# Attention and feed-forward on one core: the second chunk's units, moved one or two half steps back beside the first chunk

## The chip, the cores and the metric

The kernel runs on one core of a Trainium2 chip. The time is device microseconds (us) from one execution; a kernel's time is the median of several. The profiled execution is a single one, and its own time stands beside its span in the table below. A "clock" is the TensorE clock that the throttle granted, as a share of full speed.

Five engines work side by side, each through its own queue in order: TensorE (PE, with its weight loads as PEld), VectorE (DVE), ScalarE (ACT), GpSimd (POOL) and SyncE (SP), which here issues nearly all transfers. An instruction that waits holds everything behind it on its engine.

## The reference

Two parts follow each other. Attention: 8 batches, 8 heads of 64, 512 local tokens and 32 global ones. A local token sees the local tokens within 32 places and all global ones; a global token sees everything.

```python
s_ll = scale * np.matmul(q_l, k_l.transpose(0, 1, 3, 2))
s_ll = np.where(np.abs(pos[:, None] - pos[None, :]) <= 32, s_ll, -1e9)
a_l = sm(np.concatenate([scale * np.matmul(q_l, k_g.transpose(0, 1, 3, 2)), s_ll], axis=-1))
out_l = np.matmul(a_l, np.concatenate([v_g, v_l], axis=2))
```

Then, on the heads laid side by side (`x`, 8 x 576 x 512, in float32), a layer norm and a feed-forward with 2048 hidden columns:

```python
xn = (x - mu) / np.sqrt(var + 1e-06) * g_ln
return x + np.maximum(xn @ w_ch1, 0.0) @ w_ch2
```

## The kernel before

**Chunks and units.** The rows are cut into nine chunks: eight of 512 local rows (two halves of 256 rows each) and a last one with the 256 global rows. Chunk c's feed-forward runs on TensorE while the attention for chunk c+1 is computed in between. A local chunk's attention is eight units, one for each pair of heads and half. A unit has three parts: scores (16 small matmuls for each of two heads into two banks `sc`, L262; on VectorE the mask and row minimum, L275, four instructions; on ScalarE four exponentials, L285), transposes (four on TensorE into a bank `tp`, L299, with a copy `pt` on ScalarE, L301, for the first sixteen units; on VectorE, L307, for later ones), and values (32 matmuls into a bank `pv`, L316, a reciprocal, L327, and the scaled copy into `x` on VectorE, L328). `sc`, `tp`, `pv` and the chunk's transposes `t` (L492) share two banks. The fourth and eighth unit also finish a half: its rows are stored to DRAM (`xs`, L342) and normalised (BN_STATS L189, L191; on ScalarE L202).

**The feed-forward.** The hidden columns are cut into sixteen weights, called f0 to f15 here. For each there is a first product (`mm1`, L531, twelve 512-column matmuls into `ph`, as three passes: low weight times high x, high times low, high times high), then `hh` on ScalarE (L539) and `hl` on VectorE (L540), and a second product (`mm2`, L550, three matmuls for each of four row tiles into `acc`). `mm2` of f-1 follows `mm1` of f, so a chunk has 32 half steps: 2f is `mm1(f)`, 2f+1 is `mm2(f-1)`.

**The weights.** Beside the first chunk, each weight also arrives as a raw 64-bit tile (L165, 1 MB) and is split into a high and a low float32 part: ScalarE L138 and L139, VectorE L141, L142 and L146, ScalarE L150, VectorE L152. The raw buffers are few, so the transfer of a later weight waits until L146 of an earlier one has read its buffer. `weights_to` is called in each even half step and keeps the split four weights ahead in program order.

**What sets the order.** TensorE's queue is written out by hand from the first chunk on: `PLACES` gives for a chunk the start, the period and the offsets of a unit's three parts in half steps, and a part runs in the half step

```python
place = min(max(int(start + n * period) + o, place), 2 * NF - 1)
```

as soon as that half step's matmuls yield (three times in `mm1`, once for each row tile in `mm2`). SyncE's queue is written by hand too, in the program's order. VectorE's, ScalarE's and GpSimd's queues are ordered by a scheduler from its own costs, before the kernel runs.

Of the kernel before, what the change touches and what calls it, by code (L numbers as in the profile page):

```python
# [31 lines left out]

ON_PE = 16

PLACES = {0: (0, 3.5, (0, 2, 3)), 1: (0, 3.4, (0, 1, 4)), 7: (1, 3.5, (0, 1, 2)), 9: (1, 3.75, (0, 1, 4))}
BIG = 3.0e38


# [8 lines left out]
def attention_ffn_kernel(  # L47
# [679 lines left out]
    for c, chunk in enumerate(chunks):  # L727
# [8 lines left out]
        traced["units"] = want  # L736
        start, period, offs = PLACES.get(c, PLACES[9])
        at = {}
# [108 lines left out]
```

## Time and profile before

| | |
|---|---|
| median of 3 runs | 998.15 us (997.30, 998.15, 999.79) |
| profiled execution | 995.42 us, span 993.6 us, clock 0.983 |
| TensorE busy (matmuls) | 948.8 us, 95% |
| VectorE busy | 578.0 us, 58% |
| ScalarE busy | 314.7 us, 32% |
| raw weight transfers | 16 of 1024 KB, median 5.4 us from issue to landing |
| unit transfers (`u`) | 63 of 848 KB, median 4.7 us |

The first chunk's feed-forward stretches from about 58 to 176 us of the span. A row of the timeline has start, duration, engine, line, operation, result and operands, and in square brackets the idle time before it with what ended it. A row of the list of waits has engine, tile and line, what it waited for, and then us in total, times, longest. A piece of the chain of waits has start, duration, engine, tile and line.

### The profile page before, as it was taken

To read this page: it belongs to the slowest core of one execution; us is meant where nothing else is said; L and a number is where in the kernel's file an instruction comes from. 1 tells how busy PE (TensorE), PEld (TensorE's weight loads), DVE (VectorE), ACT (ScalarE), POOL (GpSimd) and SP (SyncE) were. 2 spreads that over 40 slices of the span, in tenths; PEclk is the share of its full clock that TensorE was granted. 3 is DMA by queue.
4 is the path that set the end of the run, shared out by engine and by line. 5 is a ranking of instruction groups with operands and counts; after the bars stand their busy time and mean duration, and the time that the engine had idled before them with its cause. 6 is when DMAs were issued, how large, how long until landed. Compare 5 with 4: busy or idle time off the path is not lost.

```text
span 993.6 us, 21066 instructions
## 1 busy us (share of the span) xinstructions
PE 948.8 (95%) x8616; PEld 717.2 (72%) x8616; DVE 578.0 (58%) x1873; ACT 314.7 (32%) x842; POOL 44.0 (4%) x150
## 2 busy tenths in 40 slices
PE   6569999999999999999999999999999989999997
PEld 4347677677777777777777777777777766766796
DVE  4589943666766666766666666766666642222311
ACT  5677743223222223222322222222222231232210
POOL 3000000000000000000000000000000000000000
PEclk9679999999999999999999999999999999999999
DMA  8565632323232224222332224222322344543110
GB/s 357 203 250 203 231 113 85 121 76 119 97 120 75 89 80 149 90 93 71 104 122 84 101 68 146 93 71 93 123 84 86 108 158 150 191 147 136 44 32 22
DMA packets 31872, 118.80 MB, mean 120 GB/s; under 512 B 4256, under 2 KB 6304, under 8 KB 27680
## 3 DMA queue, kind: packets, MB, share of 16 engines
q1 hardware_dynamic: 31776, 117.46, 34.6%
q8 instruction: 68, 1.11, 0.5%
q14 instruction: 28, 0.23, 0.1%
HBM read 99.62 MB, written 17.83 MB: 118 GB/s over the span
## 4 chain that ended last, share of the span: by engine, by line
PE 85%; DMA 3%; DVE 3%; ACT 2%; issue 1%; SPq 0%; POOL 0%; ACTq 0%; DVEq 0%
PE acc L550 37%; PE ph L531 36%; PE sc L262 4%; PE pv L316 3%; DMA raw<-in_wd 2%; PE t L492 1%; PE pv L419 1%; DMA xs<-x 1%; PE sc L371 1%; PE t L407 1%; DVE tmp L142 0%; DVE hl L540 0%; DVE pt L307 0%; DVE tmp L146 0%; ACT p L285 0%
## 5 line engine op out<-in xcount | busy, mean ns | idle before, releaser
L550 PE MATMUL acc<-w,hh 128*128 128x512 f32 x1088 | 342.7, 396 | 0.0
L531 PE MATMUL ph<-xh,w 128*128 128x512 f32 (+1 forms) x1216 | 311.7, 382 | 0.0
L307 DVE STREAM_TRANSPOSE pt<-p 32x128 f32<-32x128 f32 x768 | 232.5, 303 | 62.2 <-ACT p L285 50.1
L531 PEld LDWEIGHTS ph<-xh,w 128*128 128x128 f32 x1216 | 214.0, 188 | 49.8 <-issue 3.1
L550 PEld LDWEIGHTS acc<-w,hh 128*128 128x128 f32 x1088 | 205.7, 189 | 44.4
L550 PE MATMUL acc<-w,hl 128*128 128x512 f32 x544 | 225.7, 415 | 2.9 <-DVE hl L540 2.9
L539 ACT ACTIVATE hh<-ph 128x512 fp32r<-128x512 f32 (+1 forms) x144 | 82.3, 572 | 355.6 <-PE ph L531 354.4
L540 DVE SCALAR_TENSOR_TENSOR hl<-ph,hh 128x512 fp32r<-128x512 f32 (+1 forms) x144 | 94.3, 656 | 164.9 <-ACT hh L539 163.4
L285 ACT ACTIVATE p<-p,mn 128x128 f32<-128x128 f32 x256 | 99.7, 391 | 187.9 <-DVE mn L275 187.9
L531 PE MATMUL ph<-xl,w 128*128 128x512 f32 x512 | 143.4, 401 | 0.0
L550 PEld LDWEIGHTS acc<-w,hl 128*128 128x128 f32 x544 | 102.4, 188 | 32.7 <-issue 7.2
L531 PEld LDWEIGHTS ph<-xl,w 128*128 128x128 f32 x512 | 94.0, 188 | 27.8 <-issue 6.9
L275 DVE CUSTOM_DVE_ANT_0 p<-sc,mask 128x128 f32<-128x128 f32 x256 | 58.9, 285 | 45.4 <-PE sc L262 44.8
L262 PE MATMUL sc<-u 64*32 64x128 f32 x2048 | 58.1, 293 | 13.0 <-DMA u<-in_eu 6.2
L262 PEld LDWEIGHTS sc<-u 64*32 64x32 f32 x2048 | 32.3, 112 | 41.6 <-issue 25.1
L316 PEld LDWEIGHTS pv<-u,pt 128*32 128x32 f32 x2048 | 33.8, 113 | 28.1 <-issue 22.4
L328 DVE TENSOR_TENSOR x<-pv,ri 128x256 f32<-128x256 f32 x64 | 26.8, 420 | 43.6 <-PE pv L316 43.6
L316 PE MATMUL pv<-u,pt 128*32 128x64 f32 x2048 | 45.7, 228 | 3.1 <-ACT pt L301 3.0
L285 ACT ACTIVATION_READ_ACCUMULATOR p<-p,mn 128x1 f32 x256 | 47.9, 187 | 0.0
L326 POOL TENSOR_SCALAR ri<-sm 128x4 f32<-128x4 f32 x64 | 17.4, 272 | 585.1 <-ACT p L285 580.9
L202 ACT ACTIVATE x<-x,rs 128x512 f32<-128x512 f32 x32 | 24.8, 811 | 45.1 <-DMA xs<-x 43.5
L492 PE MATMUL t<-ident,x 128*128 128x128 f32 x136 | 23.1, 290 | 10.1 <-DVE x L207 3.9
(58 smaller groups left out, 442.0 us busy)
## 6 DMA issues: line engine op xcount, KB each, us to landing
u<-in_eu SPq DMA_DIRECT2D x63, 848.0 KB, 4.7
raw<-in_wd SPq DMA_DIRECT2D x16, 1024.0 KB, 5.4
gk<-in_gk SPq DMA_DIRECT2D x8, 1088.0 KB, 5.0
xs<-x SPq DMA_DIRECT2D x32, 256.0 KB, 5.7
ob<-xs SPq DMA_DIRECT2D x32, 256.0 KB, 3.4
out<-ob SPq DMA_DIRECT2D x32, 256.0 KB, 2.1
gv<-in_gv SPq DMA_DIRECT2D x8, 1024.0 KB, 5.0
u<-in_eu SPq DMA_DIRECT2D x1, 512.0 KB, 4.1
```

The lines of the kernel that those rows point to most:

```text
L202: nc.scalar.activation(x[:, j, :], x[:, j, :], AF.Identity, bias=rs[:, 1, j:j + 1], scale=rs[:, 0, j:j + 1],)
L262: nc.tensor.matmul(sc[h][gp, qb * P:(qb + 1) * P], self.e[hd, w * WIN:(w + 1) * WIN], self.e[hd, k0 * WIN:(k0 + 4) * WIN], start=True, sto ...
L275: nc.vector.tensor_tensor_reduce(out=self.p[:, c], in0=sc[h][:, qb * P:(qb + 1) * P], in1=masks[half, qb], scale=-QSCALE, scalar=BIG, op0= ...
L285: nc.scalar.activation(self.p[:, c], self.p[:, c], AF.Exp, bias=mn[:, c:c + 1], scale=-1.0, accum_out=self.sm[:, c:c + 1],)
L307: nc.vector.transpose(out=self.pt[rp, :, gp], in_=self.p[gp, :, rp])
L316: nc.tensor.matmul(pv[gp, qb * P + h * D:qb * P + h * D + D], self.pt[:, 2 * h + qb, gp], self.v[:, 4 * qb + g, h * D:(h + 1) * D], start= ...
L328: nc.vector.tensor_tensor(self.x[:, :, hp * P:(hp + 1) * P].rearrange("p q (h d) -> p q h d", h=2), pv[:, :256].rearrange("p (q h d) -> p ...
L492: nc.tensor.transpose(t[:, j * P:(j + 1) * P], xn[j][:, kt * P:(kt + 1) * P], ident)
L531: nc.tensor.matmul(ph[:, :n], w[:, kt, :], xx[kt][:, :n], start=(i == 0), stop=(i == 3 * KT - 1),)
L539: nc.scalar.activation(hh[:, :n], ph[:, :n], AF.Relu)
L540: nc.vector.scalar_tensor_tensor(hl[:, :n], ph[:, :n], 0.0, f32(hh[:, :n]), ALU.max, ALU.subtract)
L550: nc.tensor.matmul(acc[t], a[:, ts], w, start=(f == 0 and i == 0), stop=(f == NF - 1 and i == 2),)
```

## The change

One entry of the table is different: the first chunk's row, which places the units of the second chunk.

```diff
-PLACES = {0: (0, 3.5, (0, 2, 3)), 1: (0, 3.4, (0, 1, 4)), 7: (1, 3.5, (0, 1, 2)), 9: (1, 3.75, (0, 1, 4))}
+PLACES = {0: (2, 3.4, (0, 2, 3)), 1: (0, 3.4, (0, 1, 4)), 7: (1, 3.5, (0, 1, 2)), 9: (1, 3.75, (0, 1, 4))}
```

The scores of the eight units stood in half steps 0, 3, 7, 10, 14, 17, 21, 24 and now stand in 2, 5, 8, 12, 15, 19, 22, 25; transposes follow two and values three half steps later, as before. The scheduler gives VectorE and ScalarE another order in this chunk as a consequence; behind it, all queues are as they were. Three places follow, each first as it stood, then as it stands.

TensorE, from the last transposes of the chunk's own input (`t`) to the end of the first product of f0 (`ph` from `xh` and `xl`); `sc` are the scores of the first unit:

```order
L492 MATMUL t<-ident,x 128x128 x8
L262 MATMUL sc<-u 32x128 x16
L531 MATMUL ph<-xh_593,w 128x512 x2
L531 MATMUL ph<-xh_605,w 128x512 x2
L531 MATMUL ph<-xl_594,w 128x512 x2
L531 MATMUL ph<-xl_606,w 128x512 x2
L531 MATMUL ph<-xh_593,w 128x512 x2
L531 MATMUL ph<-xh_605,w 128x512 x2
L299 MATMUL tp<-ident,p 128x128 x4
```

```order
L492 MATMUL t<-ident,x 128x128 x4
L531 MATMUL ph<-xh_593,w 128x512 x2
L492 MATMUL t<-ident,x 128x128 x4
L531 MATMUL ph<-xh_605,w 128x512 x2
L531 MATMUL ph<-xl_594,w 128x512 x2
L531 MATMUL ph<-xl_606,w 128x512 x2
L531 MATMUL ph<-xh_593,w 128x512 x2
L531 MATMUL ph<-xh_605,w 128x512 x2
L262 MATMUL sc<-u 32x128 x16
```

The scores moved behind the first product, and two matmuls of that product now stand between the transposes.

VectorE, from an L142 of weight f4 to the scaled copy (L328) of the first unit's values. Before, `tmp_796` and `w_795` are f4 and `w_736` is f3; now `tmp_767` and `w_766` are f4 and `tmp_836` is f5; the `hl` are those of f0 and f1 before, of f1 and f2 now:

```order
L142 SCALAR_TENSOR_TENSOR tmp_796<-tmp_796,raw_745 128x1024
L146 SCALAR_TENSOR_TENSOR tmp_796<-raw_745,tmp_796 128x1024
L152 TENSOR_TENSOR w_736<-tmp_737,w_736 128x1024
L540 SCALAR_TENSOR_TENSOR hl_791<-ph_735,hh_790 128x512
L152 TENSOR_TENSOR w_795<-tmp_796,w_795 128x1024
L328 TENSOR_TENSOR x_829<-pv_830,ri_847 128x2x128
```

```order
L142 SCALAR_TENSOR_TENSOR tmp_767<-tmp_767,raw_745 128x1024
L327 RECIPROCAL ri_887<-ri_887 128x4
L540 SCALAR_TENSOR_TENSOR hl_819<-ph_765,hh_818 128x512
L146 SCALAR_TENSOR_TENSOR tmp_767<-raw_745,tmp_767 128x1024
L141 TENSOR_SCALAR tmp_836<-tmp_836 128x1024
L142 SCALAR_TENSOR_TENSOR tmp_836<-tmp_836,raw_747 128x1024
L152 TENSOR_TENSOR w_766<-tmp_767,w_766 128x1024
L540 SCALAR_TENSOR_TENSOR hl_866<-ph_834,hh_865 128x512
L146 SCALAR_TENSOR_TENSOR tmp_836<-raw_747,tmp_836 128x1024
L328 TENSOR_TENSOR x_869<-pv_870,ri_887 128x2x128
```

The three passes of f5 now stand ahead of the first unit's L328.

ScalarE, around the exponentials of the fifth unit (`p_1270` before, `p_1289` now). Before, `tmp_1427` is f12 and `tmp_1474` f13; now `tmp_1514` is f14 and `tmp_1604`, from `raw_1475`, is f15:

```order
L138 ACTIVATE tmp_1427<-raw_1266 128x1024
L139 ACTIVATE raw_1335<-raw_1335 128x1024
L138 ACTIVATE tmp_1474<-raw_1335 128x1024
L139 ACTIVATE raw_1435<-raw_1435 128x1024
L285 ACTIVATE p_1270,sm_1269<-p_1270,mn_1268 128x128 x4
L539 ACTIVATE hh_1309<-ph_1256 128x512
```

```order
L138 ACTIVATE tmp_1514<-raw_1382 128x1024
L150 CAST w_1466<-tmp_1467 128x1024
L285 ACTIVATE p_1289,sm_1288<-p_1289,mn_1287 128x128
L138 ACTIVATE tmp_1604<-raw_1475 128x1024
L285 ACTIVATE p_1289,sm_1288<-p_1289,mn_1287 128x128
L139 ACTIVATE raw_1475<-raw_1475 128x1024
L285 ACTIVATE p_1289,sm_1288<-p_1289,mn_1287 128x128 x2
```

The exponentials stood behind the work for f13; three of the four now stand behind a pass of f15, the last weight.

## The prediction

> **What bounds the kernel now.** I read the clock line first (the page's PEclk), then the three stretches of the first chunk, then TensorE's waits inside it, then the engines in order of time. The stretches, with columns time, busy time of PE, PEld, DVE, ACT, POOL, granted clock, DMA share, GB/s:
>
> ```profile
> 58.10:73.96 15.86, 13.50 (x137) 9.58 (x137) 15.23 (x33) 13.45 (x22) 0.39 (x1) 0.90 0.66 245
> 73.96:130.29 56.33, 52.92 (x457) 39.91 (x456) 52.80 (x95) 42.64 (x81) 4.62 (x7) 0.97 0.59 205
> 130.29:176.40 46.11, 46.11 (x363) 35.75 (x369) 16.82 (x42) 13.98 (x33) 1.39 (x4) 1.00 0.29 96
> ```
>
> 58.10 is where TensorE begins unit 1's scores, 176.40 where it ends the chunk's last matmul. Up to about 130 VectorE is as full as TensorE (15.23 of 15.86, 52.80 of 56.33), since it splits the weights; after that TensorE alone is full. So in the first two stretches either may end last, and in the third a delay of TensorE goes into the time one for one. TensorE's idle time there:
>
> ```profile
> PE sc L262 <- DVE xl L505: 3.9, 1, 3.9
> PE pv L316 <- ACT pt L301: 2.2, 4, 1.1
> PE sc L262 <- DVE x L328: 1.6, 3, 1.3
> PE tp L299 <- ACT p L285: 1.1, 1, 1.1
> PE acc L550 <- DVE hl L540: 0.8, 1, 0.8
> ```
>
> These rows hold all that a new order in this chunk could gain: 9.6 us, 3.9 of it ahead of unit 1's scores. Every row names an operation that queues on VectorE or ScalarE among the weights. The longest late one also costs clock:
>
> ```profile
> 121.24 0.40 PE L262 MATMUL sc<-u 64*32 64x128 f32 x2
> 122.91 1.10 PE L262 MATMUL sc<-u 64*32 64x128 f32 x30 [1.27 <-DVE x L328]
> 123.00:126.00 3.00, 3.00 (x35) 2.23 (x36) 2.97 (x11) 1.86 (x2) 0.00 (x0) 0.50 0.79 258
> ```
>
> After 1.27 us of idle the clock was 0.50 for three microseconds, worth about 1.4 us more (at 0.50, 3.0 us do the work of 1.5). No other chunk's order differs, so I cost this chunk only.
>
> **The change, part by part.** No instruction is added or removed; each of the eight units moves by one or two half steps. I write unit 1 to 8 for the second chunk's units and f0 to f15 for the weights.
>
> *The start gains.* These rows fix it:
>
> ```profile
> 58.10 1.50 PE L262 MATMUL sc<-u 64*32 64x128 f32 x32 [3.91 <-DVE xl L505]
> 56.29 0.83 ACT L504 ACTIVATE xh<-t,g_sb 128x256 fp32r<-128x256 f32 x2
> 57.57 0.87 DVE L505 SCALAR_TENSOR_TENSOR xl<-t,g_sb,xh 128x256 fp32r<-128x256 f32 x2
> 59.53 2.00 PE L531 MATMUL ph<-xh,w 128*128 128x512 f32 x4
> 76.76 0.60 PE L299 MATMUL tp<-ident,p 128*128 128x128 f32 x4
> ```
>
> The first product of f0 no longer stands behind unit 1's scores. It goes on when the last xh is there (57.1). Its eight matmuls up to the xl ones run cold at 0.46 each, as the row at 59.53 has them, and the last are warm: first product done near 61.1. The order from there costs, by these pieces of the chain of waits, 2.80 a product, 2.80 or 3.00 a group of twelve second-product matmuls, 0.60 scores, 0.58 values, 0.44 transposes:
>
> ```profile
> 136.93 0.60 PE sc L262 x32
> 137.52 3.00 PE acc L550 x12
> 140.52 2.80 PE ph L531 x12
> 143.32 0.44 PE tp L299 x4
> 146.56 0.58 PE pv L316 x32
> ```
>
> Scores to 61.75, f1's product to 64.75, f0's second product to 67.55. Unit 1's transposes wait for its exponentials: ScalarE holds them behind a weight operation that waits for f6's transfer until 65.17 (next fence; that transfer starts behind f2's L146, which does not move), then 1.03, a cast of 0.95 and four exponentials of 0.39: 68.7. Transposes to 69.2, f2's product to 72.0. Before, that point was 76.76, with 1.18 more done (unit 1's values, unit 2's scores): the new order is **3.6 us ahead**.
>
> *VectorE takes it back.* Passes of one weight; where nothing is waited for, the next instruction starts about a tenth of a microsecond before the listed end of the last, so I lay them from start to start:
>
> ```profile
> 65.17 1.16 ACT L139 ACTIVATE raw<-raw 128x1024 int32<-128x1024 uint16 x1 [0.34 <-DMA raw<-in_wd]
> 66.20 1.05 ACT L150 CAST w<-tmp 128x1024 fp32r<-128x1024 f32 x1
> 69.56 1.22 DVE L152 TENSOR_TENSOR w<-tmp,w 128x1024 fp32r<-128x1024 f32 x1
> 70.69 0.42 DVE L328 TENSOR_TENSOR x<-pv,ri 128x256 f32<-128x256 f32 x1
> 74.78 0.69 DVE L141 TENSOR_SCALAR tmp<-tmp 128x1024 f32<-128x1024 f32 x1
> 75.38 1.22 DVE L146 SCALAR_TENSOR_TENSOR tmp<-raw,tmp 128x1024 int32<-128x1024 int32 x1
> 76.52 1.22 DVE L142 SCALAR_TENSOR_TENSOR tmp<-tmp,raw 128x1024 int32<-128x1024 int32 x1
> 80.00 0.68 DVE L540 SCALAR_TENSOR_TENSOR hl<-ph,hh 128x512 fp32r<-128x512 f32 x1
> 88.22 0.28 DVE L275 CUSTOM_DVE_ANT_0 p<-sc,mask 128x128 f32<-128x128 f32 x1
> 60.27 1.23 DVE L142 SCALAR_TENSOR_TENSOR tmp<-tmp,raw 128x1024 int32<-128x1024 int32 x1
> ```
>
> A step is 0.60 for L141, 1.14 for L142, 1.13 for L146 and L152, 0.60 for hl, 0.85 for a unit's four L275, 0.35 for L328, 0.1 for the reciprocal. VectorE's order is the same until the last row ends at 61.41. From there it holds f2's L152 and f3's L146 (63.7), hl of f0 and the L275 (65.1), L141 of f4 (65.7); L152 of f3 waits for its cast until 67.15 and ends at 68.3; L142 of f4, reciprocal, hl of f1, L146 of f4 (71.3); then L141, L142 of f5, L152 of f4, hl of f2 and L146 of f5 (75.9), and only then unit 1's L328, 76.2. Unit 2's scores need the bank that it frees. TensorE is there at 73.5: **2.8 us idle**, where the row before was 0.18.
>
> On to L146 of f13: eight each of L141, L142, L146, L152 (32.0), four hl (2.4), three units' L275 (2.5), three L328 and reciprocals (1.4), 38.3 in all, and 1.65 of waits for casts and transfers: from 75.9 to 115.85. That frees the buffer of f15's transfer. In the old order it stood near 118.9, so the weights now run 3 us earlier against the units. Laying TensorE beside it I find idle 0.55 and 2.1 us at unit 2's transposes and values, 0.8 at unit 3's scores, 0.8 and 1.6 at unit 4's transposes and unit 5's scores; TensorE ends f8's product at 121.95.
>
> *Where it ends.* Unit 5's exponentials now stand in ScalarE's queue among f15's two passes. Durations:
>
> ```profile
> 64.68 4.77 DMA raw<-in_wd
> 95.67 8.71 DMA raw<-in_wd
> 121.05 1.13 ACT L138 ACTIVATE tmp<-raw 128x1024 f32<-128x1024 f32 x1
> 126.28 0.39 ACT L285 ACTIVATE p<-p,mn 128x128 f32<-128x128 f32 x1
> 130.29 0.48 PE L550 MATMUL acc<-w,hl 128*128 128x512 f32 x1
> ```
>
> The transfer of f15 starts at 115.9 and takes 4.8 to 8.7; at 5.3, near the shorter row, it lands at 121.2. L138 (1.05), an exponential (0.39), L139 (1.05), two exponentials (0.78): 124.5. Transposes of unit 5 follow 2.6 us late, end at 125.0; f7's second product (2.8), values (0.6), f9's product (3.0) and unit 6's scores (0.6) bring TensorE to f8's second product at **132.0**. Before, that was 130.29 with one set of transposes (0.44) more behind it: 129.85. So +2.2 us; all that follows is in the third stretch, where TensorE waits for nothing. VectorE's own bound, hl of f8 at 128.3, does not bind.
>
> Two unknown costs remain. Clock: the earlier stalls' slow clock is absorbed, as TensorE has 2.6 us in hand at unit 5's transposes; behind that stall it costs 0 to 1.4, and I take 0.7. The page "TensorE: Matmul & The Clock Gate" of the Trainium skill (Part 1, What's actually happening) puts the cold state behind at least one idle window of about 3.4 us. By that rule no stall here cools the array and the sum loses the 0.7; the row of 1.27 us speaks against it. Transfer: unit 6's 848 KB are queued 2.1 us ahead of f15; the 8.71 row is such a pair only 0.4 apart. I take 0.6, with 0 to 2.2 as bounds (8.71 - 4.77 - 1.7). **Sum: 2.2 + 0.7 + 0.6 = +3.5 us.** On the profiled execution (span 993.6, 995.42 us in all) that makes 998.9; the three runs' median, 998.15, lies 2.7 higher, so I forecast a median of **1001.6**.
>
> The moved loads cost nothing, and GpSimd's order is the same: unit 7's keys now wait in SyncE's queue behind the first residual load, and that behind L146 of f15 (127.7), so they land near 133.5, and the scores need them near 142. Were they late, TensorE would stop one for one.
>
> **Rivals.** *A, faster:* the head start survives. It needs VectorE and ScalarE to serve unit 2 to unit 5 with no more idle than before (2.2 + 1.6 us, less what the start removes). Then -3.6, so 994.5. For it: the weights are never what a product waits for. Against it: the laid order with L328 behind five weight passes. *B, no change:* the work of VectorE to hl of f8 is the same in both, and stalls only change place; my +2.2 without the unknown costs, less the two microseconds that hand-laid waits may err: 998 to 1000.5, say 999. *C, slower through the tail:* the last unit's values are now 8.4 us ahead of the transposes of the next chunk's input, three groups of 2.8, where the old order had 11.3.
>
> ```profile
> 156.89 0.65 PE L316 MATMUL pv<-u,pt 128*32 128x64 f32 x32
> 158.29 0.41 DVE L328 TENSOR_TENSOR x<-pv,ri 128x256 f32<-128x256 f32 x1
> 163.96 1.52 ACT L202 ACTIVATE x<-x,rs 128x512 f32<-128x512 f32 x2 [6.31 <-DMA xs<-x]
> 108.59 8.09 DMA xs<-x
> ```
>
> Values to L328 0.1, L328 0.45, store to landing 5.2, normalising 1.5: 7.3, so 1.1 us is left. Where the store takes 8.1, as the earlier one did, it is 1.8 late: 1003.4, the forecast with 1.8 on top. DMA is idle enough there (0.29) to make that unlikely.
>
> **How the numbers follow.** Forecast 0.46, A 0.18, B 0.24, C 0.12. A measurement of this kernel tells about 0.3% (3 us) from none. The forecast's own range is 999 to 1005 (costs 0 to 3.6, waits 2 either way); it lies above 1001.1 two times in three (0.30), C nearly always (0.11), B one time in ten (0.02): slower 0.43. A is faster nine times in ten: 0.17. The rest, 0.40, is within. The range 994.5 to 1006 takes in the forecast with its unknown costs, B, and C beside the forecast's centre; it leaves out half of A and C on top of a dear forecast.
>
> **What would show it.** In the new profile: f0's first product before unit 1's scores, ended near 61; a wait of unit 2's scores for L328 of 2 to 4 us near 74; a wait of unit 5's transposes for the exponentials of 1 to 4 us near 123; TensorE's idle after the first product, up to f8's second product, at 10 to 14 us (12.5 as laid, unit 1's transposes with 1.2 among them) instead of 5.7, the four lower rows of the list of waits; f8's second product at 131 to 135; no idle after it. A wait for xl that stays, f8's second product before 129, or idle ahead of the chunk's last transposes would make me wrong.

## The result, and the profile after

| | before | changed |
|---|---|---|
| median | 998.67 us (995.30 to 1000.31) | 1004.74 us (1003.20 to 1005.43) |
| profiled execution | 995.42 us, span 993.6 us | 1003.66 us, span 1001.8 us |
| TensorE's mean clock | 0.983 | 0.977 |

The changed kernel takes 1.0061 times the time of the kernel before, with an interval of 1.0036 to 1.0085: 0.6%, or 6 us, slower. A second measurement beside later experiments gave 1006.33 us and 1.0086 [1.0060, 1.0111].

Three stretches of the changed kernel answer, roughly, to the three of before (the first ends at unit 2's scores here, just behind them there): from unit 1's scores to unit 2's, to f8's second product, to the next chunk's scores (columns as before).

```profile
60.91:72.57 11.66, 11.66 (x109) 8.82 (x108) 10.83 (x21) 9.87 (x18) 0.84 (x1) 0.94 0.53 185
72.57:135.62 63.05, 54.93 (x470) 40.28 (x469) 55.62 (x96) 43.84 (x74) 3.78 (x6) 0.89 0.60 210
135.62:182.53 46.91, 46.91 (x365) 36.20 (x357) 15.75 (x49) 14.36 (x40) 1.61 (x5) 1.00 0.27 92
```

The first and the third hold no idle time of TensorE. The loss is in the second: 8.1 us idle, at a mean clock of 0.89. TensorE's waits from the first product to the chunk's end:

```profile
PE sc L262 <- DVE x L328: 4.7, 3, 2.5
PE pv L316 <- ACT pt L301: 2.3, 2, 2.0
PE ph L531 <- ACT xh L504: 1.9, 1, 1.9
PE tp L299 <- ACT p L285: 1.1, 1, 1.1
```

The wait of 3.9 us for `xl` is gone, and 1.9 us for `xh` stand there instead. What came new is the wait of the scores for L328: 4.7 us where there were 1.6. In order of time:

```profile
75.50 0.85 PE L262 MATMUL sc<-u 64*32 64x128 f32 x30 [2.54 <-DVE x L328]
76.28 0.80 PE L550 MATMUL acc<-w,hl 128*128 128x512 f32 x1
76.88 1.05 PE L550 MATMUL acc<-w,hh 128*128 128x512 f32 x2
88.07 0.65 PE L316 MATMUL pv<-u,pt 128*32 128x64 f32 x32 [2.03 <-ACT pt L301]
119.28 0.66 PE L262 MATMUL sc<-u 64*32 64x128 f32 x30 [1.80 <-DVE x L328]
128.00 0.71 PE L299 MATMUL tp<-ident,p 128*128 128x128 f32 x2 [1.11 <-ACT p L285]
135.62 0.50 PE L550 MATMUL acc<-w,hl 128*128 128x512 f32 x1
178.49 0.60 PE L492 MATMUL t<-ident,x 128*128 128x128 f32 x4
```

These are unit 2's scores and values, unit 5's scores and transposes, f8's second product and the last transposes of the next chunk's input. In the profile of before those last transposes stood here:

```profile
172.27 0.60 PE L492 MATMUL t<-ident,x 128*128 128x128 f32 x4
```

So this chunk costs 6.2 us, about the ratio of the medians. The span grew by 8.2, of which 1.5 came in the next chunk; that part is not tied to the change (last section).

The third row of the list in order of time shows something else: a pair of `hh` matmuls that takes 0.63 us at full clock took 1.05. Behind three of the idles the clock was low (the third column from the right):

```profile
75.40:80.00 4.60, 4.50 (x40) 3.41 (x41) 4.49 (x13) 3.31 (x5) 0.00 (x0) 0.63 0.90 336
88.00:97.00 9.00, 8.60 (x81) 6.00 (x82) 8.81 (x18) 5.69 (x14) 0.17 (x1) 0.62 0.64 214
119.20:124.00 4.80, 4.72 (x41) 3.65 (x42) 4.80 (x15) 1.27 (x3) 0.00 (x0) 0.64 0.97 305
```

That gave two readings of one trace. Either the units' work is queued too late on VectorE and ScalarE, as the prediction had it, and the low clock mostly falls into time that would be waited for anyway; or the idles are small and the low clock behind them is the price. The experiments were to tell these apart.

### The profile page after: what moved, and what is told of

It reads as the page before. It is cut to its first block, busy times and chain, and to the rows that moved or that the text cites. A ratio compares the mean times of both kernels' runs of the same rounds, so it can differ in the third digit from the quotient of the medians.

```text
span 1001.8 us, 21068 instructions
## 1 busy us (share of the span) xinstructions
PE 957.1 (96%) x8616; PEld 722.5 (72%) x8616; DVE 578.8 (58%) x1873; ACT 315.0 (31%) x842; POOL 43.9 (4%) x150
## 4 chain that ended last, share of the span: by engine, by line
PE 85%; DVE 3%; DMA 3%; ACT 2%; issue 1%; SPq 0%; POOL 0%; ACTq 0%; DVEq 0%
PE acc L550 37%; PE ph L531 36%; PE sc L262 4%; PE pv L316 3%; DMA raw<-in_wd 2%; PE t L492 1%; PE pv L419 1%; PE sc L371 1%; PE t L407 1%; DVE w L152 1%; ACT raw L139 1%; ACT tmp L138 1%; ACT p L285 0%; DVE hl L540 0%; DVE pt L307 0%
## 5 line engine op out<-in xcount | busy, mean ns | idle before, releaser
L285 ACT ACTIVATE p<-p,mn 128x128 f32<-128x128 f32 x256 | 99.8, 391 | 192.9 <-DVE mn L275 192.7
L275 DVE CUSTOM_DVE_ANT_0 p<-sc,mask 128x128 f32<-128x128 f32 x256 | 58.8, 285 | 45.9 <-PE sc L262 40.3
L328 DVE TENSOR_TENSOR x<-pv,ri 128x256 f32<-128x256 f32 x64 | 26.8, 419 | 47.2 <-PE pv L316 47.2
L285 ACT ACTIVATION_READ_ACCUMULATOR p<-p,mn 128x1 f32 x256 | 48.0, 188 | 0.0
L202 ACT ACTIVATE x<-x,rs 128x512 f32<-128x512 f32 x32 | 24.8, 812 | 41.1 <-DMA xs<-x 38.0
```

The costliest lines, as they stand in the source:

```text
L202: nc.scalar.activation(x[:, j, :], x[:, j, :], AF.Identity, bias=rs[:, 1, j:j + 1], scale=rs[:, 0, j:j + 1],)
L275: nc.vector.tensor_tensor_reduce(out=self.p[:, c], in0=sc[h][:, qb * P:(qb + 1) * P], in1=masks[half, qb], scale=-QSCALE, scalar=BIG, op0= ...
L285: nc.scalar.activation(self.p[:, c], self.p[:, c], AF.Exp, bias=mn[:, c:c + 1], scale=-1.0, accum_out=self.sm[:, c:c + 1],)
L328: nc.vector.tensor_tensor(self.x[:, :, hp * P:(hp + 1) * P].rearrange("p q (h d) -> p q h d", h=2), pv[:, :256].rearrange("p (q h d) -> p ...
```

## Experiments

Each ratio is against the kernel before, measured beside it.

**Which half of the edit.** The row of the table holds two numbers, a start and a period.

```diff
-PLACES = {0: (2, 3.4, (0, 2, 3)), ...
+PLACES = {0: (2, 3.5, (0, 2, 3)), ...     # start alone
...
+PLACES = {0: (0, 3.4, (0, 2, 3)), ...     # period alone
```

> Only the start of the table's row is changed (2 instead of 0), the period stays 3.5. Theory 1 (VectorE's and ScalarE's new order makes unit work late, TensorE idles for it and then runs at a low clock): VectorE's order is that of the change up to unit 4, so its wait of unit 2's scores (2 to 3 us) and unit 2's values (about 2 us) are here too, and the kernel is 4 to 7 us slower than before. Rival (the period costs, since it puts the units closer together): within 1.5 us of before.

> Only the period is changed (3.4 instead of 3.5), the start stays 0. Theory 1: no wait of unit 2's scores over 1 us at the front, as VectorE's order there is that of before; 0 to 3 us slower. Rival (the period costs): 4 to 7 us slower, with TensorE idle at units 5 and 6.

The start alone: 1003.64 us, 1.0059 [1.0033, 1.0085]. The period alone: 1000.77 us, 1.0028 [1.0005, 1.0052]. The start alone is as slow as the whole edit. The period, worth about half as much by itself, adds nothing that can be measured to the start. But the two do not lose in the same places. In the trace of the start alone the last unit's values came too late for the next chunk's transposes, as the third rival of the prediction had it: `t` waited 1.35 and 0.37 us for the normalisation L202, and the clock was 0.69 in the 5.5 us behind the first of them. By an estimate from these numbers that is about 3.3 of the 5.0 us that this trace has lost at the chunk's last transposes (177.27 against 172.27). In the changed kernel there is no such wait. So equal times do not show here that the causes are equal.

**Lighter splitting.** Here L142 and L146 are left out for f4 to f15 in both kernels, so the weights lose their third part and their sign, and VectorE has 2.27 us less to do for each.

```diff
-        nc.vector.scalar_tensor_tensor(itmp, itmp, 3, last, ...)      # L142
-        nc.vector.scalar_tensor_tensor(itmp, top, SIGN, itmp, ...)    # L146
+        if not light:
+            (both)
```

> The kernel before, with two of the three VectorE passes that join a weight's parts (L142 and L146) left out from f4 on, so that the weights are wrong and VectorE has 2.3 us less to do per weight. To be read beside the next run. Theory (the head start is real and is eaten by unit work that is late on VectorE and ScalarE): waits for VectorE shrink, 990 to 995.

> The changed kernel with the same two passes left out from f4 on. Theory: no wait after the first product over 1 us, so the head start of 3.6 us or more stays: 3 to 5 us faster than the run before this one. Rival (the new places cost by themselves, by the banks that scores share with the values of the unit before, or by the shorter distance to the chunk's last transposes): no faster than the run before this one.

Before, lightened: 995.20 us, 0.9982 [0.9962, 1.0002], just above the 990 to 995 expected. Changed, lightened: 994.07 us, 0.9960 [0.9935, 0.9985]. So with a light VectorE the changed table is no longer slower. The head start shows as 2.5 us at the end of the chunk in the two traces (163.22 against 165.68 for the first transposes of the next input) and as 1.1 us in the medians, which is less than was expected and inside the error. That points to VectorE's work; it doesn't say whether by its amount, its order or the idles that follow from it, and the lightened kernels' queues were ordered anew as well.

**The units ahead of the weights.** From f5 on, a weight's passes are queued behind the last L328 and the last exponential that stand ahead of them in the program, and the split runs three weights ahead instead of four (`SPLIT_AHEAD` 2 instead of 3). These two parts were not run apart. The same edit was made to the kernel before, and to a table in between.

```diff
-SPLIT_AHEAD = 3
+SPLIT_AHEAD = 2
...
-                yield from split_weights(ap, ahead.pop(0), *wts[f])
+                with ExitStack() as behind:
+                    for ins in last.values() if f > 4 else ():
+                        behind.enter_context(tc.issue_after(ins.ins))
+                    for _ in split_weights(ap, ahead.pop(0), *wts[f]):
+                        pass
+                yield
```

> The changed table, and one more edit: from weight f5 on, each weight's passes on VectorE and ScalarE are queued behind the unit work (L328, exponentials) that stands before them in the program, and the splitting stands one weight later in the program. Same instructions. Theory 1 (unit work queued late behind weights is the cause): TensorE's idle between the first product and f8's second product falls from 8 us to under 4, the clock stays at 1.00 there, and the time is 994 to 999. Rival (VectorE's pace, set by the weights' transfers, is the cause, whatever the queue order): weights are later still, TensorE waits for hl or for weights instead, 1002 to 1008.

> The kernel before with the same edit to the queues as the run before this one. Theory 1: the 3.4 us of waits for L328, copies and exponentials in the old order go too, and its low clock at 123 us: 993 to 997, but the 3.9 us wait ahead of unit 1's scores stays. Rival (transfers set the pace): 998 to 1003.

> Start 1, period 3.4, and the queue order in which weights from f5 on stand behind the unit work ahead of them. Unit 1's scores still follow f0's first product, but all values come one half step earlier than in the change, the last in half step 27 as before. Theory: head start kept, waits for L328 of about 1 us each without a low clock: 992 to 996. Rival (the queue order alone was worth it, the place of unit 1 nothing): 995 to 998, as the old places with that queue order.

| | table | median | ratio |
|---|---|---|---|
| units first, changed | (2, 3.4) | 997.33 us | 0.9994 [0.9972, 1.0017] |
| units first, before | (0, 3.5) | 995.39 us | 0.9969 [0.9945, 0.9993] |
| units first, between | (1, 3.4) | 994.41 us | 0.9968 [0.9945, 0.9992] |

The edit takes 7 us off the changed kernel and 3 us off the one before. The last two are both a little faster than either kernel of the change and not to be told apart. With units first, the changed table still trails the old one by some 2 us in the medians, inside the error. In the trace of the first of them TensorE is still idle for a good part of what it was in the changed kernel:

```profile
PE sc L268 <- DVE x L334: 4.6, 5, 1.7
PE pv L322 <- ACT pt L307: 2.6, 2, 1.4
```

These are 7.2 us of waits in shorter pieces, 4.5 of them ahead of 130 us; the fall to under 4 us up to f8's second product that was expected did not come. But its clock was 1.00 from 75 to 140 us. That spoke for the second reading, the low clock, and led to the next experiment.

**Filling the idles.** 22 throw-away matmuls of 512 columns go into the three idles ahead of unit 2's scores (9), its values (7) and unit 5's scores (6). Their result goes into a bank that the next product overwrites.

```diff
+    FILL = {(9, 0): (3, 9), (9, 2): (4, 7), (12, 0): (8, 6)}
...
+        for _ in range(n):
+            nc.tensor.matmul(early[f], ..., start=True, stop=True)
```

> The changed kernel with 22 more matmuls of 512 columns, into a bank that the next first product overwrites, on TensorE just ahead of three of its waits: 9 ahead of unit 2's scores, 7 ahead of unit 2's values, 6 ahead of unit 5's scores (about 0.23 us each, less than each wait lasts). The scheduler's order on VectorE and ScalarE stays that of the change as far as f6. Theory (idle as such is short; the low clock that follows it is most of the price): the clock is 1.00 from 75 to 97 us and from 119 to 124, and the time is 998 to 1001. Rival (VectorE's and ScalarE's pace sets f8's second product and the low clock only fills time that TensorE would wait anyway, as my prediction took it): clock 1.00 too, but the later waits grow by what the clock saved, and the time is 1003 to 1006.

998.31 us, 1.0009 [0.9986, 1.0032]: 6.4 us came back, and the clock was 1.00 in every stretch from 72 to 140 us. That looked like a proof of the second reading, and it was none. The scheduler that orders VectorE and ScalarE had answered the added matmuls with another order: from unit 2 on, the units' L285, L301 and L328 stood further ahead among the weights' passes. Two things had changed at once.

**A square.** To part them, both orders were written down instruction by instruction and held by edges between neighbours on each engine, up to the end of the first chunk.

```diff
+    def hold_order():
+        how = mybir.DependencyInfo(mybir.DependencyClass.NoSync, mybir.DependencyReason.DATA)
+        for queue, order in ((vec, ORDER[0]), (act, ORDER[1])):
+            for a, b in zip(order, order[1:]):
+                tc.add_manual_dep(queue.seen[b], queue.seen[a].name, how, reason="order")
```

The corners are: the changed kernel's order with and without the filling, and the other order with and without it. One more kernel has a single matmul in each place.

> The changed kernel with the same 22 throw-away matmuls as the filled kernel before (9 ahead of unit 2's scores, 7 ahead of unit 2's values, 6 ahead of unit 5's scores), but with VectorE's and ScalarE's order held to the changed kernel's, instruction by instruction, up to the end of the first chunk; nothing else differs, nothing is left out. In the run before the order of those engines had changed too, so its 6.4 us were not the clock's alone. Theory (the low clock is the larger part of the loss): clock 1.00 between 75 and 97 and between 119 and 126, f4's product ends 2.5 to 4.5 us earlier than the changed kernel's 95.5, f8's second product at 130 to 132.5 instead of 135.6, time 998 to 1001. Rival (the order of VectorE and ScalarE is what cost, and the clock only follows the waits): clock 1.00 all the same, but the time that the throw-away matmuls save is waited for at the next unit's scores or transposes, f8's second product at 134 or later, time 1003 to 1006.

> The same with 1 throw-away matmul in each of the three places (0.2 us each) instead of 9, 7 and 6. It has every edit of the filled kernel but the filling, so the idles of 1.5 to 2.3 us stay. Theory (a filled idle keeps the clock): the idles still turn the clock low in at least two of the three stretches (0.6 to 0.8 between 75 and 80, 88 and 97, 119 and 124), time 1002 to 1006. Rival (the edit gains by something other than the filling): as fast as the filled kernel, 998 to 1001.

> The changed kernel itself, beside the two filled ones on one chip. 1003 to 1006 by its 1004.74 before. The idles ahead of unit 2's scores and values and of unit 5's scores come again at 2.5, 2.0 and 1.8 us, since VectorE's and ScalarE's work does not depend on the clock; if the low clock depends on how long TensorE was idle alone, the same three stretches are low again (0.62 to 0.64), and if it depends on when within some other period the idle falls, another subset of them is, with a clock loss of 3 to 7 us up to f8's second product.

> The fourth corner of a square. The changed kernel without any throw-away matmul, with VectorE's and ScalarE's order of the first filled kernel (998.31 us) held instruction by instruction up to the end of the first chunk; TensorE's, GpSimd's and SyncE's orders differ from that kernel's by the 22 matmuls alone. From unit 3 on that order lets the units' L285, L301 and L328 pass the weights' next passes: the exponentials of units 3, 4 and 5 stand ahead of the next L138 or L150 instead of between and behind them. Order theory (what costs in the changed kernel is the units' work queued behind the weights' passes; the fill alone, in the changed kernel's order, gave 1002.9 against 1006.3): 998 to 1000.5, f8's second product before 132, unit 4's transposes, unit 4's values and unit 5's transposes without a wait over 1 us, and the idles ahead of unit 2's scores and values, which lie before the two orders part or just behind, as in the changed kernel at 2 to 3 us each. Clock theory (the fill was what gave the 6.4 us, the order came along): 1003 to 1006, with the clock low behind the unfilled idles and f8's second product at 134 or later. Halves: the two add, 1000.5 to 1003.

| | idles left | idles filled |
|---|---|---|
| the changed kernel's order | 1004.74 us, 1.0061 [1.0036, 1.0085]; again 1006.33 us, 1.0086 [1.0060, 1.0111] | 1002.90 us, 1.0066 [1.0043, 1.0090] |
| the other order | 998.76 us, 1.0000 [0.9981, 1.0020] | 998.31 us, 1.0009 [0.9986, 1.0032] |

One matmul in each place, in the changed kernel's order: 1004.53 us, 1.0074 [1.0046, 1.0101]. That kernel has the edges too, so the edges by themselves don't make a kernel faster.

The order decides. By the medians it is worth 6 to 7.6 us without filling and 4.6 with it; by the ratios, which compare each kernel with the one before beside it, 6 to 8.6 and 5.7. Undoing it brings the changed kernel back to the time before. The filling is worth 0.5 us in the other order and 1.8 to 3.4 us in the changed kernel's by the medians, and by the ratios -0.9 and -0.5 to 2.0; none of these is outside the error, so a part of up to some 3 us for the low clock is not excluded. But the theory that the low clock is the larger part fell, by the first row of this table and then by the second. Which of the instructions that changed places matters was not tried one by one; the traces below name two.

The profile of the filled kernel in the changed kernel's order shows why a fuller clock did not help. (It is of a long execution, 1007.36 us, so it is read for places and not for its time. In this kernel and the next all of VectorE's and ScalarE's instructions have line 98, through which their order was recorded, and TensorE's lines are shifted.) The first two rows are stretches of TensorE with its busy time, clock, DMA share and GB/s; the others are unit 4's transposes and values, two of unit 5's transposes, and f8's second product.

```profile
72.97:119.00 46.03, 40.29 (x346) 1.00 0.63 217
119.00:129.00 10.00, 7.20 (x60) 1.00 0.68 232
111.22 0.33 PE L331 MATMUL tp<-ident,p 128*128 128x128 f32 x1 [1.47 <-ACT p L98]
116.30 0.65 PE L348 MATMUL pv<-u,pt 128*32 128x64 f32 x32 [1.95 <-ACT pt L98]
127.09 0.33 PE L331 MATMUL tp<-ident,p 128*128 128x128 f32 x1 [1.25 <-ACT p L98]
128.51 0.72 PE L331 MATMUL tp<-ident,p 128*128 128x128 f32 x2 [1.09 <-ACT p L98]
137.68 0.49 PE L584 MATMUL acc<-w,hl 128*128 128x512 f32 x1
```

The clock is full up to 129, and TensorE reaches unit 4's scores 2.7 us earlier than in the changed kernel (102.95 against 105.63). What was saved there is waited for again at units 4 and 5. Behind the waits at unit 5's transposes the clock is low after all, 0.81 from 129 to 138, so the filling did not end the low clock in this trace; it moved it to a place where nothing was filled.

With the order undone and the idles left, the same engines look like this at unit 5. First the changed kernel, VectorE's L146 of f13, L328 of unit 4 and the first L275 of unit 5, then ScalarE's exponentials of unit 5 with L138 and L139 of f15 between them:

```profile
117.68 1.22 DVE L146 SCALAR_TENSOR_TENSOR tmp<-raw,tmp 128x1024 int32<-128x1024 int32 x1
118.81 0.42 DVE L328 TENSOR_TENSOR x<-pv,ri 128x256 f32<-128x256 f32 x1
122.67 0.28 DVE L275 CUSTOM_DVE_ANT_0 p<-sc,mask 128x128 f32<-128x128 f32 x1
...
123.05 0.40 ACT L285 ACTIVATE p<-p,mn 128x128 f32<-128x128 f32 x1 [3.07 <-DVE mn L275]
125.00 1.12 ACT L138 ACTIVATE tmp<-raw 128x1024 f32<-128x1024 f32 x1 [1.46 <-DMA raw<-in_wd]
126.03 0.39 ACT L285 ACTIVATE p<-p,mn 128x128 f32<-128x128 f32 x1
126.41 1.16 ACT L139 ACTIVATE raw<-raw 128x1024 int32<-128x1024 uint16 x1
127.83 0.41 ACT L285 ACTIVATE p<-p,mn 128x128 f32<-128x128 f32 x1
```

Then the kernel with the order undone, the same instructions: unit 4's L328, unit 5's first L275, f13's L146, and the first and last exponential of unit 5:

```profile
111.59 0.42 DVE L98 TENSOR_TENSOR x<-pv,ri 128x256 f32<-128x256 f32 x1 [0.38 <-PE pv L345]
116.71 0.28 DVE L98 CUSTOM_DVE_ANT_0 p<-sc,mask 128x128 f32<-128x128 f32 x1
117.56 1.22 DVE L98 SCALAR_TENSOR_TENSOR tmp<-raw,tmp 128x1024 int32<-128x1024 int32 x1
...
117.88 0.39 ACT L98 ACTIVATE p<-p,mn 128x128 f32<-128x128 f32 x1
119.04 0.39 ACT L98 ACTIVATE p<-p,mn 128x128 f32<-128x128 f32 x1
```

L146 of f13 stands at the same time in both, 117.68 and 117.56. The weights were not late in one and early in the other. But unit 4's L328 runs 7 us earlier and unit 5's exponentials end 9 us earlier, since they no longer stand behind f13's passes and f15's transfer. TensorE there:

```profile
76.34 0.67 PE L291 MATMUL sc<-u 64*32 64x128 f32 x30 [2.97 <-DVE x L98]
118.42 1.48 PE L328 MATMUL tp<-ident,p 128*128 128x128 f32 x4 [0.32 <-ACT p L98]
122.88 0.65 PE L345 MATMUL pv<-u,pt 128*32 128x64 f32 x32 [0.18 <-ACT pt L98]
127.06 0.50 PE L579 MATMUL acc<-w,hl 128*128 128x512 f32 x1
169.90 0.60 PE L521 MATMUL t<-ident,x 128*128 128x128 f32 x4
```

These are all its waits from unit 2's scores to the chunk's end. f8's second product begins 8.6 us before the changed kernel's, in single traces; the medians are 6 to 7.6 apart. The wait of 2.97 us at unit 2's scores, about the changed kernel's 2.54, is still there, with a low clock of some three microseconds behind it. It costs nothing against the time before: the head start pays for it. What costs in the changed kernel is what comes behind it.

## Why the prediction was right, and where its size was off

- **The forecast** was slower by 3.5 us with a median of 1001.6 us, in a range of 994.5 to 1006. It came to 6.1 us and 1004.74: right in sign and mechanism, short by 3.1. It lies inside the range, but that range takes in no change as well; of the forecast's own range, 999 to 1005, it is the upper edge.
- **The start gains.** The first product ended at 60.9 (forecast near 61) and unit 2's scores were at TensorE's head at 72.6 (forecast 73.5): some 4.5 us ahead instead of 3.6, as unit 1's transposes did not wait.
- **VectorE takes it back.** Unit 1's L328 began at 75.03, forecast 75.9 (76.2 is its end), and unit 2's scores waited 2.54, forecast 2.8. The idles behind it were laid at 5.9 us up to unit 5's scores (0.55, 2.1, 0.8, 0.8, 1.6) and were 4.4 (2.03, 0.33, 0.25, 1.80).
- **The largest term that was too small** is the one from there to L146 of f13, "38.3 in all, and 1.65 of waits": 39.95. It took 43.8 (75.03 to 118.81). VectorE's waits in that stretch:

```profile
DVE w L152 <- ACT w L150: 3.1, 3, 1.6
DVE tmp L141 <- ACT tmp L138: 0.7, 2, 0.5
DVE hl L540 <- ACT hh L539: 0.2, 1, 0.2
```

  That is 4.0 instead of 1.65, mostly for casts behind late transfers. The other 1.5 lie in steps that are longer than they were laid: L142 begins 0.72 behind its own L141, for instance (80.50 and 81.22), where 0.60 was laid. Less the 0.9 that it began earlier, f13's L146 came 3.0 us late. In the second trace of the same kernel the waits were 1.6 and the stretch 41.2, so it differs by 2.6 us between two executions. The low clock of TensorE need not be there to stretch it: with the clock full, in the filled kernel of the same order, it was again 43.7 (75.79 to 119.50).
- **It is not the only one.** Four traces have the changed kernel's order. In us, with the forecast's two unknown costs behind the plus signs:

  | | forecast | profiled execution | second trace | one matmul each | filled |
  |---|---|---|---|---|---|
  | unit 1's L328 begins at | 75.9 | 75.0 | 75.5 | 75.4 | 75.8 |
  | from there to the end of f13's L146 | 39.95 | 43.8 | 41.2 | 42.1 | 43.7 |
  | from there to L138 of f15 | 5.3 + 0.6 | 6.2 | 7.1 | 6.5 | 6.0 |
  | from there to the end of unit 5's exponentials | 3.3 | 3.2 | 3.2 | 3.3 | 3.2 |
  | from there to f8's second product | 7.5 + 0.7 | 7.4 | 9.7 | 7.4 | 8.9 |
  | f8's second product at | 133.3 | 135.6 | 136.7 | 134.5 | 137.7 |

  The second row was too small in all four, by 1.2 to 3.9 us. The last step was short where the clock behind unit 5's transposes stayed full, and long where it was low (0.55 in the second trace, 0.81 in the filled kernel). On average f8's second product came 2.8 us behind the forecast, which is the size that was missing; how it is made up differs from one execution to the next.
- **Where it ends.** In the profiled execution the steps held from there. f15's transfer took 5.96 us, forecast 5.3 and 0.6 for contention. Unit 5's exponentials stood among f15's passes as laid, 3.2 us from L138 to the last, forecast 3.27. f8's second product came at 135.62; 132.0, 0.6, the 3.0 of the last point and nothing for the clock make 135.6.
- **Clock.** The sentence that the earlier stalls' slow clock is absorbed was in doubt for five experiments and stood in the end, as far as can be measured: filling the idles in the same order brought nothing outside the error. The 0.7 behind the stall at unit 5's transposes was not needed in the profiled execution, where that clock stayed full; in the second trace it was 0.55 there and the last step 2.2 us longer than laid, beyond the bounds of 0 to 1.4. So the term is a chance, not a constant, and its upper bound was too low.
- **Rivals.** A, that the head start survives, needed VectorE and ScalarE to serve the units with no more idle; with the lightened split and with the order undone it does survive up to the chunk's end (2.5 and 2.4 us by two pairs of traces), but the medians show 1 us or none. B, no change, is out by the interval. C, a late tail, is seen in the trace of the start alone and not in the changed kernel: its last transposes have no idle ahead of them.
- **What would show it.** Four of the six signs came: the first product ahead of unit 1's scores and ended near 61, unit 2's scores waiting 2.5 us, unit 5's transposes waiting 1.1 us (at the lower edge), no idle behind f8's second product. Two missed: f8's second product came at 135.62, just past 131 to 135, and TensorE's idle was 8.1 us where 10 to 14 were forecast. The low clock took part of that idle's place: 54.93 us of work at 0.89 lose about 6 us by an estimate from the stretch, and with the 8.1 that is more than the 12.5 laid.

Why the scheduler gives the changed table the worse order stays open; it orders by its own costs, and 22 matmuls more were enough to give another.

## What to carry to other kernels

A hand-written order of one engine does not keep the order of the engines that a scheduler fills: after a move there, look first at where the moved work's consumers stand among the background work (here weights that are not needed yet) on the other engines, and price the stall by what stands ahead of them. An experiment that adds or drops instructions may change those orders too; compare them, and hold them fixed, before its time is given to the cause that it was built for. Work that shares an engine with a prefetch can be worth queueing ahead of it: with the units first, and the split one weight later, the kernel before gained 0.3%.

## What the runs showed of the hardware

**When the clock goes low.** Idles of 1.27 us (before), 1.80, 2.03 and 2.54 us (changed kernel) had a low clock behind them; 2.99 us in the second trace of the changed kernel had none in the stretch behind it, while 2.45 us in the same trace had (0.76 from 88 to 95 us):

```profile
76.01 0.66 PE L262 MATMUL sc<-u 64*32 64x128 f32 x30 [2.99 <-DVE x L328]
76.61 0.50 PE L550 MATMUL acc<-w,hl 128*128 128x512 f32 x1
76.94 0.62 PE L550 MATMUL acc<-w,hh 128*128 128x512 f32 x2
88.06 1.08 PE L316 MATMUL pv<-u,pt 128*32 128x64 f32 x32 [2.45 <-ACT pt L301]
89.08 2.07 PE L531 MATMUL ph<-xh,w 128*128 128x512 f32 x4
```

The second trace also has an idle of 1.26 us at unit 5's scores, with a clock of 1.00 behind it, where the 1.27 us of before had 0.50. So the length of the idle alone doesn't decide it. The page "TensorE: Matmul & The Clock Gate" of the Trainium skill (Part 1, What's actually happening) puts the low state behind at least one idle window of about 3.4 us; none of these idles was that long, and for them the measurement differs. What does decide it stays open.

**The same idle, two prices.** In the next chunk every trace has an idle of 2.19 or 2.20 us at f0's second product. In the trace of before the clock stayed full behind it, in that of the changed kernel it did not (0.61 from 191 to 195):

```profile
191.19 0.50 PE L550 MATMUL acc<-w,hl 128*128 128x512 f32 x1 [2.19 <-DVE hl L540]
193.75 1.06 PE L550 MATMUL acc<-w,hh 128*128 128x512 f32 x2
```

The chunk took 110.3 us from its last transposes to the next chunk's before (172.27 to 282.59) and 111.8 in the changed kernel (178.49 to 290.32). But the kernel before with the units first, whose next chunk is ordered alike, also took 111.8 (167.94 to 279.78), and the first filled kernel, with the changed table, 110.3 (171.00 to 281.30). Of the fourteen traces four have 110.3 and ten 111.8, either table among both. So these 1.5 us do not go with the table; they look like a draw of each execution, though no kernel was seen with both. Two single traces can differ by that much for no reason in the edit.
